# Down projection by Strassen's seven products, and matmuls issued as 64-column halves, in a long-convolution and gated-MLP kernel

## The chip, the cores and the metric

The kernel runs on one core of one Trainium2 chip. The metric is device time in microseconds (us) of one execution; lower is better. A core has a matrix engine (PE, with its weight loads shown as PEld), VectorE (DVE), ScalarE (ACT), GpSimd (POOL) and SyncE (SP), which here only starts DMA transfers. The engines run their own instruction queues in order and meet through semaphores. PE reads from SBUF and writes to PSUM, which has eight banks of 512 float32 columns on 128 partitions; POOL does not touch PSUM in this kernel.

## What is computed

```python
batch, seq, d_model, filter_order = 4, 12480, 128, 64
...
h_filt = (np.maximum(pos_emb @ w1, 0.0) @ w2) * np.exp(-0.01 * pos)[:, None]
u = x * v
y = irfft(rfft(u, n=2*S) * rfft(h_filt, n=2*S))[:, :S, :]
z = (x * y).reshape(B * S, D)            # 49920 tokens of 128 channels
h = z @ w_in                             # w_in: 128 x 2048
return (h * np.cos(h)) @ w_out           # w_out: 2048 x 128
```

Everything is float32 (the two large weights arrive as float64 and are converted on the chip). The first half is a causal convolution of each channel with a long filter; the second is an MLP with the activation h·cos(h).

## The kernel before

The convolution is made of small Fourier matrices, in five kinds of work per batch element: the product u = x·v and its even and odd sums (`u_multiply`, `u_sums`, on POOL in the middle of the kernel), a forward stage (`f1_mm`, line 410), a second stage with the product by the filter's transform (`f2_mm`, line 451, and `f2_product`, lines 474 to 477), an inverse stage (`i1_mm`, line 482) and a last one (`i2_mm`, line 507), whose result `i2_out` multiplies by x and stores to a scratch array `zd` in DRAM. The filter's own transform and batch element 0 as far as `i1` are done first, alone.

From then on the MLP and the convolution are interleaved by hand (`manual_schedule`: each queue has the order in which the code issues). The tokens are cut into 98 row groups (`NALL`), 512 tokens each but for the first and the last, and the 2048 hidden channels into 16 chunks of 128 (`NFC`). One step of the main loop is one chunk of one row group: 1568 steps. Step i issues, in this order:

- `moe_up`: one matmul of 128 weight columns by 512 tokens into a PSUM tile `ph` (line 746), then on ACT the rounding to whole turns, `k` (line 749), and on DVE the remainder `f` (line 751);
- `moe_down` for step i − LAG: one matmul of 512 tokens that adds to the accumulator `acc` (line 768, also shown as `cv` when the accumulator lies in a bank of the convolution);
- `moe_act` for step i − 1: the sine on ACT (`cs`, line 757) and the product with `ph` on DVE (`gt`, line 759). This is the last reader of that step's `ph`;
- at some steps: `moe_turn` (four transposes of the next row group's tokens, line 129, through a `ph` tile and an ACT copy, line 740), `moe_back` (four transposes of the result, line 129, through a `ph` tile and the ACT copy `ob`, line 783), loads and stores;
- then as much work of the convolution as the accounting in `owed` asks for: every step adds 1, every yield of the convolution costs its own number of steps.

Each float32 matmul is recorded as two matmul records and two weight loads; a transpose as one of each. In the main loop PSUM holds four `ph` tiles (`ps_h`), one accumulator and three banks of the convolution (`ps_c`). The steps after the convolution's end are called the tail here.

Where the last stage of one batch element runs (`inverse_units`), the products u of the next one are made beside it. `u_units` has a pool of `bufs` buffers for x and `bufs − 1` for v (`xt`, `vt`); the load of a tile waits until POOL has multiplied the tile that held its buffer. SP's one queue issues these loads, the loads of `tm` and `xs` for the last stage, the stores to `zd`, the loads `zb` of the MLP and the stores of the result, all in program order.

Of the kernel before, what the change touches and what calls it, by code (L numbers as in the profile page):

```python
# [33 lines left out]
def kernel(  # L34
# [74 lines left out]
    LAG = 4  # L109
# [15 lines left out]
    tw_w = const.tile([KE, 2, N1], F32, name="tw_w")  # L125

# [26 lines left out]
    def float32_join(dst, raw, power, high):  # L153
# [6 lines left out]
        if dst.space == DRAM:  # L160
# [5 lines left out]
                 for c in range(0, DFF, WCOL)]  # L166
    out_pieces = [(slice(c, c + WCOL // D), out_words[:, c:c + WCOL // D, :, :])
                  for c in range(0, NFC, WCOL // D)]
# [239 lines left out]
    def f1_mm(ps, u, b, i):  # L408

        nc.tensor.matmul(ps[0:KE, i * 2 * N1:(i + 1) * 2 * N1], u[:, b, 0:KE, i],  # L410
                         c1[0:u.shape[0], :, :].rearrange("p r k -> p (r k)"),
                         start=True, stop=True)
# [32 lines left out]
    def f2_mm(ps, w, k1, i, filt=False):  # L445
# [4 lines left out]
        if not filt:  # L450
            nc.tensor.matmul(pi, w[:, i, :], parts[0:KE, :, k], start=True, stop=True)  # L451
        elif k < KF:
            both = ftile[0:KE, :, k:k + N1 + 1:N1, :].rearrange("p b r i -> p r b i")
            nc.tensor.matmul(pi, w[:, i, :], both, start=True, stop=True)
        else:
            for r, src in enumerate((ftile[0:KE, :, k, :], above[0:KE, :, k - KF, :])):
                nc.tensor.matmul(pi[:, r], w[:, i, :], src, start=True, stop=True)  # L457
# [22 lines left out]
    def i1_mm(ps, b, i):  # L480
        for r in range(2):
            nc.tensor.matmul(  # L482
                ps[0:N1, (i * 2 + r) * N2:(i * 2 + r + 1) * N2],
                parts[0:N2, r, :, b, i],
                cs[:, r, :], start=True, stop=True)
# [10 lines left out]
    def i2_mm(ps, t, g, part):  # L496
        for i in range(part * G // 2, (part + 1) * G // 2):
# [8 lines left out]
            for r, place in enumerate(places):  # L506
                nc.tensor.matmul(ps[0:R, i * D:(i + 1) * D], t[:, i, r, :],  # L507
                                 slots[0:N1, :, place, :], start=(r == 0), stop=(r == 1))

    def i2_out(pool, ps, xs, b, g):  # L510
        if b == 0:
            yield
        zs = pool.tile([R, 2, UA, D], F32, name="zs")
        nc.vector.tensor_tensor(
            zs[:, :, :, :].rearrange("p h n d -> p (h n d)"), ps[0:R, :],
            xs[:, :, :].rearrange("p h n -> p (h n)"), op=ALU.mult)
        z = zs[:, :, :, :].rearrange("p h n d -> p (h n) d")
# [150 lines left out]
    def i2_units(bank, b, bufs):  # L668

        with tc.tile_pool(name="back", bufs=2, side="left" if b else "right") as pool:  # L670
            ts, xss = {}, {}

            def before(j):
                ts[j] = pool.tile([N1, G, 2, R], F32, name="tm", bufs=bufs)
                xss[j] = pool.tile([R, 2, UA * D], F32, name="xs", bufs=bufs)
# [15 lines left out]
    def inverse_units(bank, b):  # L691
# [6 lines left out]
        new = u_units(b + 1, 3, slots[0:R, :, :, :],  # L698
# [20 lines left out]
    ats, accs = {}, {}  # L719
# [7 lines left out]
    def moe_load(pool, n):  # L727
        m, row = rows_of(n), first_row(n)
        zb = pool.tile([P, G, D], F32, name="zb", bufs=2)
# [13 lines left out]
    def moe_up(pool, n, c):  # L743
        m = G * rows_of(n)
        ph = ps_h.tile([P, BANK], F32, name="ph")
        nc.tensor.matmul(ph[:, 0:m], w_in_sb[:, c * P:(c + 1) * P], ats[n][:, 0:m],  # L746
                         start=True, stop=True)
        k = pool.tile([P, BANK], I32, name="k")
        nc.scalar.activation(k[:, 0:m], ph[:, 0:m], AF.Identity, bias=TURNS[c % 4][0])  # L749
        f = pool.tile([P, BANK], F32, name="f", bufs=3)  # L750
        nc.vector.scalar_tensor_tensor(out=f[:, 0:m], in0=ph[:, 0:m],  # L751
                                       scalar=TURNS[c % 4][0], in1=k[:, 0:m], op0=ALU.add, op1=ALU.subtract)
        return ph, f, m, TURNS[c % 4][1] * TWO_PI

    def moe_act(pool, ph, f, m, scale):
        cs = pool.tile([P, BANK], F32, name="cs")
        nc.scalar.activation(cs[:, 0:m], f[:, 0:m], AF.Sin, scale=scale)  # L757
        gt = pool.tile([P, BANK], F32, name="gt", bufs=4)
        nc.vector.tensor_tensor(gt[:, 0:m], ph[:, 0:m], cs[:, 0:m], op=ALU.mult)  # L759
        return gt  # L760

    def moe_down(n, c, gt):
        if c == 0:

            accs[n] = bank() if made[0] == B * NG and n % 2 else \
                ps_acc.tile([P, BANK], F32, name="acc")
        m = G * rows_of(n)
        nc.tensor.matmul(accs[n][:, 0:m], w_out_sb[:, c, :], gt[:, 0:m],  # L768
                         start=(c == 0), stop=(c == NFC - 1))

    def moe_evict(pool, n):
        m = G * rows_of(n)
        ot = pool.tile([D, BANK], F32, name="ot", bufs=1)
        nc.scalar.copy(out=ot[:, 0:m], in_=accs.pop(n)[:, 0:m])
        return ot

    def moe_back(pool, n, ot):
        m = rows_of(n)
        pt = ps_h.tile([P, BANK], F32, name="ph")
        for i in range(G):  # L780
            transpose(pt[0:m, i * D:(i + 1) * D], ot[:, i * m:(i + 1) * m], ident)
# [18 lines left out]
    with tc.manual_schedule():  # L800
        with tc.tile_pool(name="psum", bufs=8, space=PSUM) as psum, \
# [96 lines left out]
            for kept, here in ((rowsd, rows), (twd, tw_t)):  # L898
# [4 lines left out]
            w_out_sb = wpool.tile([P, NFC, D], F32, name="w_out_sb")  # L903
            nc.sync.dma_start(w_in_sb[:, :], wind[:, :])
            beside(i1_units(bank), [(w_out_sb[:, c, :], w) for c, w in out_pieces], 2.0 * math.pi,
                   some_groups)

        ps_acc = ctx.enter_context(tc.tile_pool(name="ps_acc", bufs=1, space=PSUM))
        ps_h = ctx.enter_context(tc.tile_pool(name="ps_h", bufs=4, space=PSUM))
# [24 lines left out]

        conv = convolutions()
# [11 lines left out]
        hidden, gates, ots, obs = {}, {}, {}, {}  # L947
        for i in range(len(steps) + LAG):
            if i < len(steps):
# [5 lines left out]
                hidden[i] = moe_up(mpool, n, c)  # L955
            if i >= LAG:
                pn, pc = steps[i - LAG]
                moe_down(pn, pc, gates.pop(i - LAG))
                if pc == NFC - 1:
                    ots[pn] = moe_evict(mpool, pn)  # L960
            if 0 <= i - 1 < len(steps):
                gates[i - 1] = moe_act(mpool, *hidden.pop(i - 1))
# [41 lines left out]
```

## Time and profile before

| what | us |
|---|---|
| median of 3 runs | 3737.86 (3736.82 to 3740.14) |
| the profiled execution's own time | 3736.99 |
| its span, first to last instruction | 3734.9 |

Busy time by stretch of the span, in us; the granted TensorE clock is 1.00 in all of them and 0.995 over the span:

| stretch | what runs beside the MLP | PE | DVE | POOL |
|---|---|---|---|---|
| 340 to 600 | last stage of element 0, u of element 1 | 259.36 | 192.04 | 97.43 |
| 600 to 740 | forward stage | 140.00 | 106.41 | 1.47 |
| 740 to 1040 | second stage and product | 300.00 | 251.32 | 69.58 |
| 1040 to 1180 | inverse stage | 140.00 | 102.10 | 0.00 |
| 1180 to 1400 | last stage of element 1, u of element 2 | 219.81 | 140.96 | 86.54 |
| 1990 to 2210 | last stage of element 2, u of element 3 | 220.00 | 141.15 | 86.61 |
| 2660 to 2940 | inverse and last stage of element 3 | 280.00 | 185.19 | 0.00 |
| 2940 to 3730 | nothing: the tail | 789.74 | 577.54 | 0.00 |

Busy time of matmuls counts from the start of a record to its modelled end, so overlapping records are merged; how densely PE works is read from the distance between the starts of two records.

### The profile page before, as it was taken

Reading aid. Unit: us, or ns where it says so; the run is one execution under the profiler, and the core shown is the slowest. Engines: PE = TensorE matmul, PEld = TensorE weight load, DVE = VectorE, ACT = ScalarE, POOL = GpSimd, SP = SyncE. Lnnn points to the kernel's source line nnn. Section 1 sums busy time; section 2 is a strip of 40 time slices with the busy share of each in tenths; the row PEclk is TensorE's granted clock in tenths of the full one; section 3 lists DMA queues with packets and bytes.
Section 4 is the critical chain, followed back from the end, with each engine's and each line's share of the span. In section 5 each row is a group of like instructions: output and inputs, shape, how many; then the busy total and the mean of one; then the engine's idle time right before and its main releaser. Section 6 shows DMA issues by size and latency. Waiting matters only on the chain.

```text
span 3734.9 us, 46660 instructions
## 1 busy us (share of the span) xinstructions
PE 3681.9 (99%) x13546; PEld 2109.8 (56%) x13546; DVE 2805.7 (75%) x5330; ACT 2294.6 (61%) x4660; POOL 714.6 (19%) x1005
## 2 busy tenths in 40 slices
PE   8898999999999999999999999999999999999999
PEld 6777555555566556555565556555666544444444
DVE  8887777788876667788876667888775677777776
ACT  5757666655555557655555567655554566666666
POOL 6666340022201430122102420122000000000000
PEclk9999999999999999999999999999999999999999
DMA  5263551022203650122104630122106200000000
GB/s 168 65 184 114 159 163 38 25 76 76 67 17 95 177 149 12 47 74 79 49 18 136 182 102 16 56 80 76 40 15 182 68 23 17 17 23 18 18 21 15
DMA packets 209494, 276.10 MB, mean 74 GB/s; under 512 B 17111, under 2 KB 146535, under 8 KB 209111
## 3 DMA queue, kind: packets, MB, share of 16 engines
q1 hardware_dynamic: 209239, 273.12, 25.0%
q8 instruction: 109, 1.79, 0.2%
q14 instruction: 146, 1.20, 0.1%
HBM read 193.64 MB, written 79.42 MB: 73 GB/s over the span
## 4 chain that ended last, share of the span: by engine, by line
PE 95%; DVE 1%; DMA 1%; ACT 1%; POOL 1%; issue 1%; SPq 0%; DVEq 0%; ACTq 0%; POOLq 0%
PE ph L746 36%; PE acc L768 31%; PE cv L507 6%; PE cv L768 5%; PE cv L482 4%; PE cv L451 3%; PE cv L410 3%; PE ph L129 2%; PE ps L410 2%; PE ps L451 1%; PE ps L482 1%; DMA wd<-w 1%; DVE slots L492 0%; PE ps L457 0%; DVE ftile L367 0%
## 5 line engine op out<-in xcount | busy, mean ns | idle before, releaser
L749 ACT ACTIVATE k<-ph 128x512 int32<-128x512 f32 (+1 forms) x1568 | 932.8, 595 | 1237.0 <-PE ph L746 1236.5
L751 DVE SCALAR_TENSOR_TENSOR f<-ph,k 128x512 f32<-128x512 f32 (+1 forms) x1568 | 1080.1, 689 | 792.8 <-ACT k L749 779.5
L746 PE MATMUL ph<-at,w_in_sb 128*128 128x512 f32 (+1 forms) x3136 | 1596.2, 590 | 0.6 <-ACT at L740 0.6
L768 PE MATMUL acc<-gt,w_out_sb 128*128 128x512 f32 (+1 forms) x2688 | 1369.4, 591 | 0.0
L759 DVE TENSOR_TENSOR gt<-ph,cs 128x512 f32<-128x512 f32 (+1 forms) x1568 | 1064.1, 679 | 60.5 <-ACT cs L757 60.4
L757 ACT ACTIVATE cs<-f 128x512 f32<-128x512 f32 (+1 forms) x1568 | 973.2, 621 | 0.6 <-DVE f L751 0.6
L768 PEld LDWEIGHTS acc<-gt,w_out_sb 128*128 128x128 f32 x2688 | 508.0, 189 | 642.4 <-issue 630.0
L746 PEld LDWEIGHTS ph<-at,w_in_sb 128*128 128x128 f32 x3136 | 553.6, 190 | 330.7 <-issue 239.8
L477 POOL TENSOR_TENSOR slots<-slots,t 120x256 f32<-120x256 f32 x384 | 281.1, 738 | 1149.2 <-DVE t L476 623.1
L507 PEld LDWEIGHTS cv<-slots,tm 96*104 96x104 f32 x1920 | 239.2, 169 | 100.2 <-issue 86.2
L398 POOL TENSOR_TENSOR xt<-xt,vt 104x256 f32<-104x256 f32 x228 | 165.8, 747 | 514.5 <-DMA vt<-in_v_dram 513.3
L507 PE MATMUL cv<-slots,tm 96*104 96x128 f32 x1920 | 251.5, 273 | 5.2 <-POOL tm L300 5.0
L768 PE MATMUL cv<-gt,w_out_sb 128*128 128x512 f32 (+1 forms) x448 | 224.0, 583 | 0.0
L482 PEld LDWEIGHTS cv<-cs,slots 120*96 120x96 f32 x1536 | 176.6, 167 | 67.1 <-issue 65.2
L482 PE MATMUL cv<-cs,slots 120*96 120x120 f32 x1536 | 183.1, 266 | 0.0
L404 POOL TENSOR_TENSOR slots<-xt 104x256 f32<-104x256 f32 x210 | 157.2, 756 | 94.1 <-PE cv L507 78.2
L451 PEld LDWEIGHTS cv<-slots,w 124*120 124x120 f32 x576 | 103.6, 184 | 124.3 <-issue 110.2
L451 PE MATMUL cv<-slots,w 124*120 124x256 f32 x576 | 173.0, 380 | 0.0
L410 PEld LDWEIGHTS cv<-c,slots 104*124 104x124 f32 x768 | 132.7, 192 | 64.8 <-issue 61.0
L410 PE MATMUL cv<-c,slots 104*124 104x192 f32 x768 | 150.8, 326 | 0.0
L768 PEld LDWEIGHTS cv<-gt,w_out_sb 128*128 128x128 f32 x448 | 85.0, 190 | 103.2 <-issue 99.5
L492 DVE TENSOR_TENSOR slots<-cv,other 96x240 f32<-96x240 f32 x384 | 132.9, 393 | 1.4 <-ACT other L490 1.1
(129 smaller groups left out, 2307.4 us busy)
## 6 DMA issues: line engine op xcount, KB each, us to landing
h<-hd SPq DMA_DIRECT2D x144, 240.0 KB
tm<-td SPq DMA_DIRECT2D x96, 312.0 KB
xt<-in_x_dram SPq DMA_DIRECT2D x120, 208.0 KB
vt<-in_v_dram SPq DMA_DIRECT2D x120, 208.0 KB
xs<-in_x_dram SPq DMA_DIRECT2D x120, 208.0 KB
zd<-zs SPq DMA_DIRECT2D x119, 208.0 KB
zb<-zd SPq DMA_DIRECT2D x96, 256.0 KB
w<-wd SPq DMA_DIRECT2D x144, 116.2 KB
```

The source lines that it names most:

```text
L398: engine.tensor_tensor(xt[:, half, :], xt[:, half, :], vt[:, half, :], op=ALU.mult)
L410: nc.tensor.matmul(ps[0:KE, i * 2 * N1:(i + 1) * 2 * N1], u[:, b, 0:KE, i], c1[0:u.shape[0], :, :].rearrange("p r k -> p (r k)"), start=Tr ...
L451: nc.tensor.matmul(pi, w[:, i, :], parts[0:KE, :, k], start=True, stop=True)
L477: nc.gpsimd.tensor_tensor(y[:, r], y[:, r], t[:, r], op=op)
L482: nc.tensor.matmul(ps[0:N1, (i * 2 + r) * N2:(i * 2 + r + 1) * N2], parts[0:N2, r, :, b, i], cs[:, r, :], start=True, stop=True)
L507: nc.tensor.matmul(ps[0:R, i * D:(i + 1) * D], t[:, i, r, :], slots[0:N1, :, place, :], start=(r == 0), stop=(r == 1))
L746: nc.tensor.matmul(ph[:, 0:m], w_in_sb[:, c * P:(c + 1) * P], ats[n][:, 0:m], start=True, stop=True)
L749: nc.scalar.activation(k[:, 0:m], ph[:, 0:m], AF.Identity, bias=TURNS[c % 4][0])
L751: nc.vector.scalar_tensor_tensor(out=f[:, 0:m], in0=ph[:, 0:m], scalar=TURNS[c % 4][0], in1=k[:, 0:m], op0=ALU.add, op1=ALU.subtract)
L757: nc.scalar.activation(cs[:, 0:m], f[:, 0:m], AF.Sin, scale=scale)
L759: nc.vector.tensor_tensor(gt[:, 0:m], ph[:, 0:m], cs[:, 0:m], op=ALU.mult)
L768: nc.tensor.matmul(accs[n][:, 0:m], w_out_sb[:, c, :], gt[:, 0:m], start=(c == 0), stop=(c == NFC - 1))
```

## The change

The down projection no longer multiplies each chunk by all 128 output channels and 512 tokens. Two chunks are taken together, and the 2 × 2 blocks (two chunks by two halves of the channels, two chunks by two halves of the tokens) are multiplied by Strassen's seven products instead of eight. The sums of weights are made once, on POOL; the sums of the gated tokens (`moe_sums`) on POOL for each pair of chunks; the sums of the results when the accumulators are emptied (`moe_evict`, now in two halves). Each product has 64 weight columns and 256 tokens and is issued as two matmuls of 128 tokens that write partitions 0 to 63 and 64 to 127. In the main loop every other matmul, those of the convolution and the up projection, is also issued as two matmuls of at most 64 columns; the inverse stage's 96 rows become 97, so that its second half has 33. The transposes stay whole. The accumulators take two banks, so `ps_h` has three; after the convolution's end every other `ph` tile lies in one of its banks. The lag from up to down grows from 4 to 6 steps, the loads of u have one buffer less, and some tiles are worked on in place.

```diff
-    LAG = 4
+    LAG = 6
...
+    def mm(dst, left, right, start=True, stop=True):
+        n = dst.shape[0]
+        for lo, hi in ((0, CB), (CB, n)) if tiled[0] else ((0, n),):
+            nc.tensor.matmul(dst[lo:hi], left[:, lo:hi], right, start=start, stop=stop)
...
-            nc.tensor.matmul(
-                ps[0:N1, (i * 2 + r) * N2:(i * 2 + r + 1) * N2],
-                parts[0:N2, r, :, b, i],
-                cs[:, r, :], start=True, stop=True)
+            n = max(N1, CB + CB // 2 + 1) if tiled[0] else N1
+            mm(ps[0:n, (i * 2 + r) * N2:(i * 2 + r + 1) * N2],
+               slots[0:N2, b, r * N1:r * N1 + n, i], cs[:, r, :])
...
-                xss[j] = pool.tile([R, 2, UA * D], F32, name="xs", bufs=bufs)
+                xss[j] = pool.tile([R, 2, UA * D], F32, name="xs", bufs=bufs + 1)
...
-        new = u_units(b + 1, 3, slots[0:R, :, :, :],
+        new = u_units(b + 1, 2, slots[0:R, :, :, :],
...
-        zb = pool.tile([P, G, D], F32, name="zb", bufs=2)
+        zb = pool.tile([P, G, D], F32, name="zb", bufs=1)
...
-        ph = ps_h.tile([P, BANK], F32, name="ph")
-        nc.tensor.matmul(ph[:, 0:m], w_in_sb[:, c * P:(c + 1) * P], ats[n][:, 0:m],
-                         start=True, stop=True)
+        late = made[0] == B * NG and c % 2
+        ph = bank() if late else ps_h.tile([P, BANK], F32, name="ph")
+        mm(ph[:, 0:m], w_in_sb[:, c * P:(c + 1) * P], ats[n][:, 0:m])
...
+    def moe_sums(pool, n, gt):
+
+        half = G // 2 * rows_of(n)
+        ts = pool.tile([P, 4, BANK // 2], F32, name="ts")
+        t = [ts[:, i, 0:half] for i in range(4)]
+        b11, b21 = gt[:, 0, 0:half], gt[:, 1, 0:half]
+        nc.gpsimd.tensor_tensor(
+            ts[:, 0:2, 0:half], gt[:, :, half:2 * half],
+            gt[:, 0, 0:2 * half].rearrange("p (h n) -> p h n", h=2), op=ALU.subtract)
+        nc.gpsimd.tensor_tensor(t[2], t[1], b11, op=ALU.add)
+        nc.gpsimd.tensor_tensor(t[3], b21, t[2], op=ALU.subtract)
+        return b11, b21, gt[:, 1, half:2 * half], t
+
+    def moe_down(n, pair, second, b11, b21, b22, t):
+
+        r = rows_of(n)
+        if pair == 0:
+            sums[n, second] = ps_acc.tile([P, 4, P], F32, name="acc" + "ab"[second])
+        acc = sums[n, second]
+        todo = ((3, 6, b22), (0, 1, t[1]), (1, 4, t[0]), (2, 3, t[3])) if second else \
+            ((0, 0, b11), (2, 2, b21), (1, 5, t[2]))
+        for i, (place, weight, right) in enumerate(todo):
+            for h in range(2):
+                nc.tensor.matmul(acc[h * CB:(h + 1) * CB, place, 0:r],
+                                 w_out_sb[:, pair, weight, :], right[:, h * r:(h + 1) * r],
+                                 start=(pair == 0 and i == 0), stop=(pair == NFC // 2 - 1),
+                                 skip_group_check=True)
...
+        if not second:
+            ot = pool.tile([P, 6, P], F32, name="ot", bufs=1)
+            nc.scalar.copy(out=ot[:, 2, 0:r], in_=acc[:, 0, 0:r])
+            nc.vector.tensor_tensor(ot[:, 0:2, 0:r], acc[:, 1:3, 0:r], twice(ot[:, 2, 0:r]),
+                                    op=ALU.add)
+            return ot
+        nc.vector.tensor_tensor(ot[:, 2:4, 0:r], acc[:, 0:2, 0:r], twice(ot[:, 0, 0:r]),
+                                op=ALU.add)
+        nc.vector.tensor_tensor(ot[:, 4:6, 0:r], acc[:, 2:4, 0:r], ot[:, 2:4, 0:r], op=ALU.add)
+        nc.vector.tensor_tensor(ot[:, 0, 0:r], acc[:, 1, 0:r], ot[:, 2, 0:r], op=ALU.add)
         return ot
...
+            for dst, first_, second_, op in ((4, 1, 3, ALU.add), (5, 4, 0, ALU.subtract),
+                                             (1, 0, 1, ALU.subtract), (6, 2, 5, ALU.subtract)):
+                nc.gpsimd.tensor_tensor(w_out_sb[:, :, dst, :], w_out_sb[:, :, first_, :],
+                                        w_out_sb[:, :, second_, :], op=op)
...
-        ps_h = ctx.enter_context(tc.tile_pool(name="ps_h", bufs=4, space=PSUM))
+        ps_h = ctx.enter_context(tc.tile_pool(name="ps_h", bufs=3, space=PSUM))
...
+        tiled[0] = True
...
-                moe_down(pn, pc, gates.pop(i - LAG))
-                if pc == NFC - 1:
-                    ots[pn] = moe_evict(mpool, pn)
+                moe_down(pn, pc // 2, pc % 2, *gates[i - LAG - pc % 2])
+                if pc >= NFC - 2:
+                    ots[pn] = moe_evict(mpool, pn, pc % 2, ots.get(pn))
             if 0 <= i - 1 < len(steps):
-                gates[i - 1] = moe_act(mpool, *hidden.pop(i - 1))
+                moe_act(*hidden.pop(i - 1))
+                pn, pc = steps[i - 1]
+                if pc % 2:
+                    gates[i - 2] = moe_sums(mpool, pn, pairs.pop(i - 2))
```

`f1_mm`, `f2_mm` and `i2_mm` call `mm` in place of `nc.tensor.matmul` and are otherwise as before. `moe_back` transposes four blocks of `ot` into places that put the channel halves together again.

## The prediction

> **What bounds the kernel now.** I read the share of each engine first, then the chain that ended last, then the order of events in the tail, then the stretches.
>
> ```profile
> PE 3681.9 (99%) x13546; PEld 2109.8 (56%) x13546; DVE 2805.7 (75%) x5330; ACT 2294.6 (61%) x4660; POOL 714.6 (19%) x1005
> ...
> PE 95%; DVE 1%; DMA 1%; ACT 1%; POOL 1%; issue 1%; SPq 0%; DVEq 0%; ACTq 0%; POOLq 0%
> PE ph L746 36%; PE acc L768 31%; PE cv L507 6%; PE cv L768 5%; PE cv L482 4%; PE cv L451 3%; PE cv L410 3%; PE ph L129 2%; PE ps L410 2%; PE ps L451 1%; PE ps L482 1%; DMA wd<-w 1%; DVE slots L492 0%; PE ps L457 0%; DVE ftile L367 0%
> ```
>
> PE is the bound: it never waits in the main loop, and the down projection (L768, as acc and cv) is 36% of the chain, as much as the up projection. The timeline of PE in the tail shows how densely it works:
>
> ```profile
> 3003.23 1.02 PE L746 MATMUL ph<-at,w_in_sb 128*128 128x512 f32 x2
> 3004.09 1.02 PE L768 MATMUL cv<-gt,w_out_sb 128*128 128x512 f32 x2
> 3004.95 0.60 PE L129 MATMUL ph<-ident,zb 128*128 128x128 f32 x4
> 3005.39 1.02 PE L746 MATMUL ph<-at,w_in_sb 128*128 128x512 f32 x2
> ```
>
> The first column is the start. A float32 matmul of 512 columns takes 0.86 us from its start to the next one's, 0.429 per record; a transpose of 128 columns 0.44/4 = 0.110. A record's modelled duration is 0.592 (mean of L746), so 0.16 us of each lies under its successor. A step of up and down is 2 x 0.858 = 1.717 us.
>
> The stretches, in columns PE, PEld, DVE, ACT, POOL, show where another engine is near. They are: u made beside the last stage; the forward stage; the second stage; the tail.
>
> ```profile
> 1180.00:1400.00 220.00, 219.81 (x875) 125.90 (x874) 140.96 (x222) 116.81 (x211) 86.54 (x121) 1.00 0.57 167
> 1400.00:1550.00 150.00, 150.00 (x533) 91.23 (x532) 114.60 (x223) 103.95 (x228) 2.22 (x3) 1.00 0.06 18
> 1550.00:1840.00 290.00, 290.00 (x852) 149.31 (x851) 243.47 (x473) 170.23 (x309) 68.77 (x93) 1.00 0.25 73
> 2940.00:3730.00 790.00, 789.74 (x2024) 363.47 (x2022) 577.54 (x901) 540.36 (x984) 0.00 (x0) 1.00 0.07 18
> ```
>
> **The change, part by part.** *Seven products.* For a pair of chunks PE had two down matmuls, 4 x 0.429 = 1.716 us. It now has 7 x 2 = 14 matmuls of 64 columns by 128 tokens, 28 records of 0.109 (the transposes, and 0.111 for the 128-token records of L507 below): 3.05 us one after the other, 1.526 if the two halves stream side by side. No row of before has two matmuls at once, so the trace bounds this from both sides: −0.19 us a pair, x 784 pairs = −149 us, or +1.34 x 784 = +1050. The same question hangs on the up projection (0 or +0.858 x 1568 = +1345) and the convolution's halves (0 or at most +758, the summed busy time of L507, L482, L410 and L451 of cv). I take side by side, −149: two halves use separate columns and partitions, and the weight loads, which are already hidden under 0.102 us records at 96 columns, become shorter. No row shows which side is nearer; this is a judgement.
>
> *Transposes stay whole.* Four times per row group, 392 times, PE changes between 64-column halves and the whole array. Bounds: nothing, or the 0.16 us tail plus a weight load of 0.19 (L746's PEld) bare each time, 0.35. I take 0.25, 98 us, of which some 40% falls into the waits below: +60 (0 to 137).
>
> The page "TensorEngine Tiling (Array Packing)" of the Trainium skill, section Key Properties, says that changing the tiling mode drains TensorE; no row of before shows such a change, and by that rule alone the zero end would fall away.
>
> *Three ph tiles instead of four.* With an up at 2999.80, its gt ends at 3004.56 (3003.88 + 0.68): the tile is held for 4.76 us, 2.8 steps, because gt stands on DVE behind the next step's f. Three tiles cover three steps (5.15), but twice per row group four transposes take one of them. In the order up A, transposes, up B, up C, C needs A's tile and is due 2 x 1.717 + 0.44 = 3.87 us after A: it waits 0.9. In the changed program's order the up behind the result's transposes even waits, in 68 of 98 row groups, for the copy of those same transposes (0.16 of tail and 0.58, L783), which comes to about as much. The wait holds all of PE, including the convolution queued behind. Before the tail there are 1118 steps, 70 row groups, 140 such places: 126 us bare. Work of the convolution issued in between (on average 0.5 us a step: 2585 us from the first up at 355 to 2940, by 1118 steps, less 1.77 with transposes) covers part, and some places lie in stretches that POOL sets. I take +80 (0 to 140). The tail has six tiles and pays nothing.
>
> *Sums on POOL.* A 128x256 POOL operation is 0.728 (L150) to 0.738 (L477); 512 columns are not shown, between one and two of these; by the slope from 0.623 to 0.640 at 208 columns (L300) about 1.28. A pair costs 1.28 + 2 x 0.74 = 2.76 us (2.2 to 2.95), 1.38 a step. In the tail that is 2.76 of 3.4 us: hidden. In the second stage POOL has 69 + 139 x 1.38 = 261 of 290: just hidden. Where u is made, POOL has 87 + 96 x 1.38 = 219 of 220, and 97 + 119 x 1.38 = 262 of 260: full at the old pace. The 311 steps of these three stretches gain nothing: 311 x 0.095 = +30. And what waits there waits in POOL's queue ahead of the sums:
>
> ```profile
> 1254.43 1.42 POOL L398 TENSOR_TENSOR xt<-xt,vt 104x256 f32<-104x256 f32 x2 [2.87 <-DMA vt<-in_v_dram]
> ...
> 1256.17 0.46 SPq L379 DMA_DIRECT2D vt<-in_v_dram  x1
> 1256.85 1.05 PE L507 MATMUL cv<-slots,tm 96*104 96x128 f32 x8
> ...
> 1261.10 1.41 POOL L398 TENSOR_TENSOR xt<-xt,vt 104x256 f32<-104x256 f32 x2 [2.60 <-DMA vt<-in_v_dram]
> ```
>
> Already now v's load is issued when the last product is done (1256.17) and the next product starts 4.93 us later, on its landing, every 6.7 us. With one buffer less, and 4.1 us of sums per such round queued on POOL around those products, the round becomes 4.9 + 0.4 of issue + 1.4 of products + part of the sums, 7 to 8 us. Behind the waiting product stand the sums, for which PE's down waits; behind the waiting load on SP stand xs, tm (for which L507 waits), zd and zb. 90 rounds x 0 to 1.1 us: +50 (0 to 100).
>
> *Emptying the accumulators.* Per row group ACT's copy of 512 (0.585, L774) becomes one of 128, and DVE gets three operations of 256 columns (0.415, L476) and one of 128 (about 0.28 by the same slope): 1.5 us, 0.10 a step. In the tail DVE has 0.68 + 0.69 + 0.10 = 1.47 of a step of 1.7; it hides under PE and would cost its 150 us only if DVE became the bound. The four weight sums come once, before the first down needs them, and lag 6 delays only the end, by POOL's chain and the longer emptying: +5.
>
> **Sum:** 3734.9 − 149 + 30 + 60 + 80 + 50 + 5 = 3811; with the 2.1 us outside the span (3736.99) and 0.9 to the median, **3814 us**, slower by 2%. Its own range is 3745 to 3900.
>
> **The rivals.** *Faster, 3670.* One mechanism: PE keeps the saving because its waits are covered. It needs the ph waits and width changes nearly free: the convolution's work between ups already fills 0.5 of the 0.9 us, and a width change at 0.1 us costs 39. 3738 − 149 + 30 + 39 + 10 = 3668. It decides once ph waits, width changes and POOL together cost less than about 140. For it: everything else is off the chain. Against it: nothing in the two timelines stands between a transpose and the next up where no convolution is due.
>
> *Halves start in order, 4200.* In before every record starts after the one ahead of it in the program. A matmul is two records, so the second half of an up (429 ns records) runs on while the first half's column group has finished; if a record may not start before the one ahead, a following product half of 0.109 waits 0.429 − 0.109 = 0.32 us, each step: 1568 x 0.32 = 502. PE would be slower, so POOL and ph waits shrink to some 80 with the width changes: 3738 − 149 + 502 + 80 = 4171, and up to 4250.
>
> The page "TensorE: Matmul & The Clock Gate" of the Trainium skill, Part 3, section "What overlaps and what doesn't", speaks for this: matmuls start and end in program order and only weight loads are pulled ahead; the same section reports tiles running concurrently. By its order rule the sum is the 4171 just given, by free column groups 3814. No run here shows either.
>
> *The array does not share.* If small matmuls need the 0.102 us that the tightest load-and-matmul pair shows (L482), each half by itself: 28 x 0.102 = 2.86 for 1.716, +896, and L507 and L482 doubled, 1920 x 0.111 + 1536 x 0.102 = +370: 5000. If nothing streams side by side: 3738 + 1050 + 1345 + 758 = about 6900.
>
> **Numbers.** Slower as summed 0.38; faster 0.29; in between, no measurable change, 0.05; in order 0.17; not shared 0.11. So faster 0.29, same 0.05, slower 0.66, where 0.2% is about what a measurement of this kernel can tell. The time is the likeliest case's. The range leaves out what is under 3655 and over 4200.
>
> **What would show it.** In the tail: starts of two ups 3.2 to 3.4 us apart per pair would confirm sharing, 3.9 the order, over 5 neither. Around L129's records: an idle of PE before and after. At PE's waits: ups waiting for DVE's gt, before the tail only. In 1180 to 1400: POOL above 95% and PE idle, waiting for ts. I am wrong in kind if PE's pair takes longer than 3.43 in the tail, and wrong in size if waits for ph are absent.

## The result and the profile after

| | us | against before |
|---|---|---|
| before, median of 4 runs | 3738.61 (3736.82 to 3740.14) | |
| after, median of 4 runs | 3947.86 (3946.23 to 3959.36) | 1.0566, 95% interval 1.0545 to 1.0587 |
| after, span of the profiled execution | 3947.6 | |

The change costs 209 us. The page of the changed kernel, engine shares and the chain by engine:

```profile
PE 3703.9 (94%) x40298; PEld 2595.6 (66%) x40298; DVE 2903.3 (74%) x5722; ACT 2281.0 (58%) x4660; POOL 2838.1 (72%) x3361
...
PE 67%; POOL 11%; DMA 5%; DVE 5%; issue 2%; ACT 1%; SPq 1%; POOLq 0%; ACTq 0%; DVEq 0%
```

In after, line 132 is the helper `mm` and 785 the seven products; 768, 771 and 772 are the sums on POOL; 754 makes `f`, 760 is the product `gt`; 404 multiplies x by v, 410 makes the sums of u, 481 and 482 are the second stage's product with the filter.

PE had 99% of the span and 95% of the chain. It now has 94% and 67%, so it waits; POOL has gone from 19% of the span to 72%, and with DMA it takes 16% of the chain.

Where the time went is read by stage. A stage begins with the first matmul of its kind in the trace; the numbers are the distances to the next stage's first matmul, in us, and "last" runs from element 3's last stage to the last up, so it holds the tail. The later rows are the experiments below.

| kernel | u made beside the last stage, three times | second stage, three times | forward and inverse stages, all six | last | median |
|---|---|---|---|---|---|
| before | 250 / 229 / 236 | 296 / 293 / 294 | 858 | 933 | 3739 |
| after | 271 / 288 / 299 | 324 / 319 / 322 | 856 | 919 | 3948 |
| e1, before in halves | 259 / 238 / 244 | 306 / 303 / 303 | 870 | 957 | 3829 |
| e3, before with three ph | 262 / 237 / 244 | 314 / 310 / 309 | 877 | 1004 | 3905 |
| e2, after without the sums | 260 / 233 / 240 | 305 / 301 / 301 | 847 | 918 | 3754 |
| e4, after, three sets of u | 272 / 286 / 297 | 324 / 319 / 321 | 856 | 917 | 3947 |
| e6, after, two buffers of t | 271 / 294 / 296 | 306 / 302 / 302 | 856 | 918 | 3897 |
| e7, after, u's products on DVE | 284 / 266 / 266 | 324 / 321 / 321 | 849 | 914 | 3903 |
| e10, after, tm from ACT's queue | 271 / 264 / 268 | 324 / 320 / 322 | 855 | 911 | 3881 |
| e11, t and tm | 271 / 260 / 270 | 306 / 302 / 301 | 856 | 911 | 3829 |
| e12, t, tm, products on DVE | 271 / 280 / 274 | 305 / 302 / 302 | 851 | 911 | 3848 |
| e13, the same and a fourth ph | 270 / 253 / 261 | 338 / 332 / 325 | 1173 | 911 | 4213 |
| e15, t, tm, three sets of u | 270 / 238 / 246 | 305 / 302 / 301 | 856 | 911 | 3781 |
| e16, the same, products on DVE | 270 / 236 / 243 | 305 / 302 / 301 | 853 | 911 | 3772 |
| e9, seven products in the tail only | 255 / 229 / 236 | 297 / 293 / 294 | 859 | 917 | 3730 |
| e14, e9 with lag and buffers as before | 255 / 229 / 236 | 296 / 293 / 294 | 859 | 917 | 3730 |

After loses 143 us in the stages where u is made (858 − 715) and 82 in the second stages (965 − 883); the forward and inverse stages together and the last part are faster.

The tail shows the products themselves. The timeline of PE there, ups and downs:

```profile
3502.30 1.03 PE L132 MATMUL ph<-at,w_in_sb 128*64 128x512 f32 x4
3503.16 0.61 PE L785 MATMUL acca<-gt,w_out_sb 128*64 128x128 f32 x8
3503.59 0.39 PE L785 MATMUL acca<-ts,w_out_sb 128*64 128x128 f32 x4
3503.81 1.03 PE L132 MATMUL cv<-at,w_in_sb 128*64 128x512 f32 x4
3504.67 0.39 PE L785 MATMUL accb<-gt,w_out_sb 128*64 128x128 f32 x4
3504.89 0.82 PE L785 MATMUL accb<-ts,w_out_sb 128*64 128x128 f32 x12
3505.54 1.03 PE L132 MATMUL ph<-at,w_in_sb 128*64 128x512 f32 x4
```

The first column is the start. An up of two halves takes 0.86 us, as one whole matmul did, and the 28 product records 0.65 + 0.87 = 1.52 us: two halves do stream side by side. A pair of chunks takes 3505.54 − 3502.30 = 3.24 us instead of 3.43. The saving is real, and it is the stages with the convolution that give it back.

The waits there, first in the stage where element 2's u is made (1216 to 1504), with total us, times and the longest:

```profile
PEld cv L132 <- DMA tm<-td: 39.9, 18, 4.9
POOL ts L768 <- PE accb L785: 37.7, 21, 4.8
PE cv L132 <- DMA tm<-td: 35.6, 18, 4.6
...
POOL xt L404 <- DMA vt<-in_v_dram: 23.2, 13, 2.6
```

and in a second stage (748 to 1072):

```profile
DVE t L481 <- POOL slots L482: 36.7, 33, 2.6
POOL ts L768 <- PE accb L785: 35.5, 34, 2.4
...
PE ph L132 <- DVE gt L760: 16.5, 22, 1.6
```

The same two kinds of stage in before, 1180 to 1400 and 740 to 1040, have no wait for `tm` and none of DVE for POOL among their longest. The longest of each:

```profile
POOL xt L398 <- DMA vt<-in_v_dram: 234.2, 29, 164.4
```

```profile
POOL slots L477 <- DVE t L476: 203.7, 91, 3.8
```

In the first stage of after, PE stands for a load of the last stage's matrices, which SP issues in order behind the loads of x and v; in the second, DVE stands for POOL in the product with the filter, where POOL had waited for DVE before, and PE stands for DVE's last read of a `ph` tile. POOL itself is not full: the stretches, with the columns PE, PEld, DVE, ACT, POOL, then the granted clock:

```profile
1240.00:1500.00 260.00, 219.32 (x2480) 156.91 (x2476) 139.23 (x232) 108.92 (x198) 198.23 (x246) 0.95 0.47 132
1640.00:1940.00 300.00, 280.74 (x2844) 176.15 (x2840) 237.26 (x481) 162.79 (x294) 243.84 (x289) 1.00 0.24 68
```

POOL has 198 of 260 and 244 of 300 us, while PE stands idle for 41 and 19. So the question for the experiments was whether POOL's work is too much or only stands in the wrong order.

### The profile page after: what moved, and what is told of

Same layout as the page of the kernel before. It is cut to its first block, busy times and chain, and to the rows that moved or that the text cites. A ratio compares the mean times of both kernels' runs of the same rounds, so it can differ in the third digit from the quotient of the medians.

```text
span 3947.6 us, 101170 instructions
## 1 busy us (share of the span) xinstructions
PE 3703.9 (94%) x40298; PEld 2595.6 (66%) x40298; DVE 2903.3 (74%) x5722; ACT 2281.0 (58%) x4660; POOL 2838.1 (72%) x3361
## 4 chain that ended last, share of the span: by engine, by line
PE 67%; POOL 11%; DMA 5%; DVE 5%; issue 2%; ACT 1%; SPq 1%; POOLq 0%; ACTq 0%; DVEq 0%
PE ph L132 23%; PE cv L132 18%; PE accb L785 14%; PE acca L785 10%; DMA tm<-td 4%; POOL ts L768 4%; PE ph L136 2%; POOL ts L771 2%; POOL ts L772 2%; DVE gt L760 2%; DVE gt L754 1%; POOL xt L404 1%; POOL slots L482 1%; POOL slots L410 1%; ACT gt L753 1%
## 5 line engine op out<-in xcount | busy, mean ns | idle before, releaser
L753 ACT ACTIVATE gt<-ph 128x512 int32<-128x512 f32 (+1 forms) x1339 | 797.7, 596 | 1347.3 <-PE ph L132 1231.3
L768 POOL TENSOR_TENSOR ts<-gt 128x512 f32<-128x512 f32 (+2 forms) x784 | 998.4, 1273 | 791.4 <-PE accb L785 737.1
L754 DVE SCALAR_TENSOR_TENSOR gt<-ph,gt 128x512 f32<-128x512 f32 (+1 forms) x1339 | 918.9, 686 | 791.1 <-ACT gt L753 779.3
L132 PE MATMUL ph<-at,w_in_sb 128*64 128x512 f32 (+1 forms) x5356 | 1414.0, 601 | 78.6 <-DVE gt L760 56.8
L759 ACT ACTIVATE gt<-gt 128x512 f32<-128x512 f32 (+1 forms) x1568 | 973.8, 621 | 32.1 <-DVE gt L754 32.1
L760 DVE TENSOR_TENSOR gt<-ph,gt 128x512 f32<-128x512 f32 (+1 forms) x1339 | 907.4, 678 | 0.3
L785 PE MATMUL accb<-ts,w_out_sb 128*64 128x128 f32 (+2 forms) x9408 | 655.1, 273 | 0.0
L772 POOL TENSOR_TENSOR ts<-gt,ts 128x256 f32<-128x256 f32 (+2 forms) x784 | 571.1, 728 | 61.5
L771 POOL TENSOR_TENSOR ts<-ts,gt 128x256 f32<-128x256 f32 (+2 forms) x784 | 570.6, 728 | 61.5
L785 PEld LDWEIGHTS accb<-ts,w_out_sb 128*64 128x64 f32 x9408 | 549.3, 138 | 0.0
```

Of the source, the lines that this page charges most:

```text
L132: nc.tensor.matmul(dst[lo:hi], left[:, lo:hi], right, start=start, stop=stop)
L753: nc.scalar.activation(turns, ph[:, 0:m], AF.Identity, bias=phase)
L754: nc.vector.scalar_tensor_tensor(out=part, in0=ph[:, 0:m], scalar=phase, in1=turns, op0=ALU.add, op1=ALU.subtract)
L759: nc.scalar.activation(part, part, AF.Sin, scale=scale)
L760: nc.vector.tensor_tensor(part, ph, part, op=ALU.mult)
L768: nc.gpsimd.tensor_tensor(ts[:, 0:2, 0:half], gt[:, :, half:2 * half], gt[:, 0, 0:2 * half].rearrange("p (h n) -> p h n", h=2), op=ALU.sub ...
```

## The experiments

### What each part costs by itself

**e1: halves alone.** Before, with every matmul of the main loop cut in two, eight products and four `ph` tiles as they were.

```diff
...
-        nc.tensor.matmul(ph[:, 0:m], w_in_sb[:, c * P:(c + 1) * P], ats[n][:, 0:m],
-                         start=True, stop=True)
+        mm(ph[:, 0:m], w_in_sb[:, c * P:(c + 1) * P], ats[n][:, 0:m])
...
-        nc.tensor.matmul(accs[n][:, 0:m], w_out_sb[:, c, :], gt[:, 0:m],
-                         start=(c == 0), stop=(c == NFC - 1))
+        mm(accs[n][:, 0:m], w_out_sb[:, c, :], gt[:, 0:m],
+           start=(c == 0), stop=(c == NFC - 1))
```

> The kernel before, with every matmul of the main loop (down too) issued as two halves of at most 64 columns and nothing else changed: eight products, lag 4, four ph tiles, no sums. It prices the halves and the changes of width around the transposes. Width theory, from the changed kernel's tail (0.245 us more around each of 196 groups of transposes than their 0.109 pitch): 3738 + 48 = 3786, and a tail step of 1.78 against 1.751 before. If the halves themselves cost anything on PE, above 3800; if the width changes explain the result, about 3940.

Measured: 3828.82 us (3826.0 to 3829.8), ratio 1.0237 (1.0222 to 1.0253), +89 us. In its tail a step takes 1.7880 us against 1.7515, which is 0.58 us for each row group of 16 steps with its two groups of transposes; over all 1568 steps that makes 57 us. The other 32 us lie in the stages with the convolution, whose matmuls are halves too. What makes those dearer was not tried.

**e3: three ph tiles alone.** Before, with `bufs=3` for `ps_h`.

```diff
-        ps_h = ctx.enter_context(tc.tile_pool(name="ps_h", bufs=4, space=PSUM))
+        ps_h = ctx.enter_context(tc.tile_pool(name="ps_h", bufs=3, space=PSUM))
```

> The kernel before with three ph tiles instead of four. My forecast's term: up to 0.9 us at 140 places before the tail, and in the tail, which has no other tiles here, at another 56: 3738 + 80 to 180 = 3820 to 3920. If the convolution's work covers the waits, 3738 to 3780, the tail alone.

Measured: 3904.5 us (3903.5 to 3905.55), ratio 1.0441 (1.0425 to 1.0457), +164 us. A tail step takes 1.9019 us; 458 x 0.1504 = 69 us of the loss is in the tail, which the changed kernel doesn't pay, since its ups use the convolution's banks there. Ahead of it 95 us are lost. The group of the ups' weight loads, with busy time, mean ns, and then the idle time before it, first in before, then here:

```profile
L746 PEld LDWEIGHTS ph<-at,w_in_sb 128*128 128x128 f32 x3136 | 553.6, 190 | 330.7 <-issue 239.8 <-DVE gt L759 15.9 <-DVE t L476 13.9
L746 PEld LDWEIGHTS ph<-at,w_in_sb 128*128 128x128 f32 x3136 | 548.5, 189 | 496.7 <-issue 155.7 <-DVE gt L759 124.1 <-ACT at L740 107.4
```

The tile comes free by DVE's `gt`, or is one that transposes hold until ACT's copy `at`: the two waits that were expected.

**e2: no sums.** After, where the products read parts of `gt` and the three POOL operations of `moe_sums` are gone.

```diff
-        nc.gpsimd.tensor_tensor(
-            ts[:, 0:2, 0:half], gt[:, :, half:2 * half],
...
-        nc.gpsimd.tensor_tensor(t[2], t[1], b11, op=ALU.add)
-        nc.gpsimd.tensor_tensor(t[3], b21, t[2], op=ALU.subtract)
-        return b11, b21, gt[:, 1, half:2 * half], t
+        return b11, b21, gt[:, 1, half:2 * half], [b11, gt[:, 0, half:2 * half], b21, b11]
```

> The changed kernel without the sums of gated tokens: the products read slices of gt in their place, so POOL has none of its 2140 us of new work; all 14 matmuls of a pair, the three ph tiles and the single u buffer stay. POOL theory: the stretches where u is made and the second stages lose their 59 and 27 us each, so 3948 - 225 = 3723 or, with the saving of 0.095 a step that comes back there, down to 3660 to 3690. Ph theory (three tiles hold PE): it stays above 3850.

Measured: 3753.92 us (3747.77 to 3758.8), ratio 1.0041 (1.0028 to 1.0053). The sums cost 3948 − 3754 = 194 us, of which 125 in the stages where u is made and 58 in the second stages. All the rest of the change together is +15 us. Nine tenths of the loss is therefore due to the sums. They do not make DVE's own work longer: `gt` (line 760) takes 678 ns in after as without the sums, and 679 in before.

### Why the sums cost that much

**e4: the third set of u buffers back.**

```diff
-        new = u_units(b + 1, 2, slots[0:R, :, :, :],
+        new = u_units(b + 1, 3, slots[0:R, :, :, :],
```

> The changed kernel with the loads of u on three buffers of x and two of v, as before. If the single v buffer makes SP's queue wait and tm late (PE waited 36 to 38 us for tm in each of two such stretches), those stretches give back most of their 59 us: 3948 - 100 = about 3850. If POOL's work alone fills them (1.38 us a step of sums beside 88 us), they stay near 280 us: 3930 to 3950.

Measured: 3947.42 us (3942.96 to 3952.84), ratio 1.0556 (1.0541 to 1.0572): nothing. Taken alone, the buffer that the change removed is not the cause. This did not yet show that it is harmless; e15 shows that it is not.

**e6: two buffers for t.** In the second stage's product POOL adds `t` to `slots` (line 482) and frees it; DVE can't write the next `t` before. POOL's addition now stands behind 2.7 us of sums.

```diff
-        t = pool.tile([N2, 2, CB, 4], F32, name="t", bufs=1 + whole)
+        t = pool.tile([N2, 2, CB, 4], F32, name="t", bufs=2)
```

> The changed kernel with two buffers for the tile t of the second stage's products instead of one, so that VectorE no longer waits there for GpSimd (108.2 us of waits in the profile of the changed kernel). If that wait is what makes the second stages 26 to 28 us longer than before, they fall by some 15 us each and the kernel to about 3900 us. If GpSimd's own work, queued in order, is the limit, VectorE's wait goes and PE's waits stay: 3940 to 3950 us, and second stages of 319 to 324 us as now.

Measured: 3896.98 us (3892.07 to 3899.2), ratio 1.0424 (1.0409 to 1.044), 51 us less. The second stages come back to 306, 302 and 302, about what they take with no sums at all (305, 301, 301). The waits in one of them (749 to 1055):

```profile
PEld ph L132 <- DVE gt L760: 6.5, 9, 0.9
```

DVE's wait for POOL is gone from the list, and the ups' wait for `gt` is small. POOL does the same work there in less time, 262 of 306 us: it was never the limit, only a queue in which a small operation stood behind large ones.

**e7: u's products on DVE.**

```diff
         new = u_units(b + 1, 2, slots[0:R, :, :, :],
-                      lambda j, half: nc.gpsimd,
+                      lambda j, half: nc.vector,
```

> The changed kernel with u's products x*v (two a round, 0.73 us each on GpSimd) on VectorE in the two stages where u is made beside the tokens' work, and in the rest as it is. GpSimd is relieved of 60 rounds x 1.46 = 88 us in these stages (VectorE was busy for 139 of 260 us there). If GpSimd's load is what makes these stages 59 to 63 us longer than before, they come back to 235 to 250 us each and the kernel to about 3850 us. If the loads' order in SyncE's queue is the cause, the wait for tm stays at some 30 us a stage: 3920 to 3950 us.

Measured: 3903.25 us (3897.0 to 3906.41), ratio 1.0441 (1.0425 to 1.0456). The edit moves the products in all three stages. It gives half of what the theory of a full POOL asked for: the two later stages fall to 266, not to 235 to 250, and the first rises from 271 to 284. In the second of the three DVE now waits 34.7 us for v. Neither theory is met.

**e10: tm's loads from ACT's queue.**

```diff
-                nc.sync.dma_start(ts[j][:, :, :, :], td[j, :, :, :, :])
+                nc.scalar.dma_start(ts[j][:, :, :, :], td[j, :, :, :, :])
```

> The changed kernel with the loads of tm issued from ScalarE's queue instead of SyncE's, where they stand behind loads of x and v whose buffers GpSimd holds. If SyncE's order is what keeps PE waiting (36 to 41 us in each of the two later stages where u is made), these waits go and the kernel falls to 3860 to 3880 us. If GpSimd's work is the limit, the wait only changes its name (PE waits for the sums or for u instead) and the time stays at 3930 to 3950 us.

Measured: 3881.18 us (3880.1 to 3885.89), ratio 1.0386 (1.0371 to 1.0402), 67 us less, nearly all that SP's order was expected to give. The waits in the same stage as above, now 1215 to 1479:

```profile
PEld acca L785 <- POOL ts L771: 20.1, 11, 3.4
PE acca L785 <- POOL ts L771: 17.3, 9, 3.2
POOL xt L404 <- DMA vt<-in_v_dram: 16.0, 9, 2.8
POOL ts L768 <- PE accb L785: 11.1, 6, 4.8
```

PE no longer waits for `tm`. What it waits for now is the sums, half as long, and POOL still stands for v.

**e11: both repairs,** the diffs of e6 and e10 together.

> The changed kernel with both repairs that helped in the stages: two buffers for t, and tm's loads from ScalarE's queue. Alone they gave 51 and 67 us. If they mend different places (second stages; stages where u is made), they add up: 3825 to 3835 us. If both only shift the same lack of GpSimd time, the sum is well under 118 us: 3850 us or more.

Measured: 3829.09 us (3828.37 to 3834.39), ratio 1.0247 (1.0233 to 1.0261). 51 and 67 add up, 3948 − 118 = 3830, to within the spread of the runs. They mend two places that don't touch: the table has e6's second stages and, nearly, e10's stages where u is made.

**e12: both, and u's products on DVE in the later two stages.**

```diff
-                      lambda j, half: nc.gpsimd,
+                      lambda j, half: nc.vector if b else nc.gpsimd,
```

> As the run with both repairs, and u's products on VectorE in the later two of the three stages where u is made. If what is left there (264 and 268 us, against 233 and 240 with no sums) is GpSimd being late with the sums, these two fall to 240 to 250 us and the kernel to 3785 to 3805 us, some 40 us above the run without sums (3754). If it is VectorE's or the loads' turn to be late, nothing is gained: 3825 us or more.

Measured: 3848.11 us (3843.52 to 3850.65), ratio 1.0293 (1.0279 to 1.0307): 19 us lost where some 35 were to be won. The waits in the stage from 1200 to 1480:

```profile
DVE xt L404 <- DMA vt<-in_v_dram: 57.0, 23, 3.9
...
POOL ts L768 <- DVE gt L760: 28.1, 12, 3.2
PE ph L132 <- DVE gt L760: 25.9, 20, 3.8
```

The wait for v went with the product to DVE, an engine on which every step depends: `gt` stands behind it, then the ups and the sums. POOL has 180 us of work in 280, so time on POOL was not what was short.

**e15: both repairs and three sets of u,** the diffs of e4, e6 and e10. What differs from e11 is that v is loaded a round ahead, and POOL's work is the same.

> As the run with both repairs (3829 us), and three sets of u tiles instead of two, which loads v a round earlier. In the changed kernel alone the third set gave nothing; there PE stood behind tm's loads. If GpSimd's waits for v (22 us in a stage where u is made) are what is left of the loss there, these stages fall from 260 and 270 to 240 to 250 us and the kernel to 3785 to 3805 us. If GpSimd's own time is the limit (225 us of work in 260), its idle time only moves: 3815 to 3830 us.

Measured: 3780.88 us (3780.19 to 3782.33), ratio 1.0115 (1.01 to 1.013), 48 us under e11. The edit that gave nothing in e4 gives 48 us after the other two. That it is `tm` that had hidden its worth is argued: in e4 PE still waits 36 us for `tm` in the second of the three stages, and `t` is used in other stages. The two later stages take 238 and 246 us, 6 and 7 more than with no sums, with POOL busy for 216 of 238. The waits in the first of them (1200 to 1440), and after it the page's chain:

```profile
POOL ts L768 <- PE accb L785: 13.0, 10, 4.8
...
PEld cv L132 <- POOL slots L410: 5.0, 2, 4.6
```

```profile
PE 82%; DVE 4%; ACT 2%; POOL 2%; issue 1%; DMA 1%; ACTq 0%; SPq 0%; POOLq 0%; DVEq 0%
```

No wait for v or `tm` is on this list any more, and POOL has fallen from 11% of the chain to 2%. The 4.6 us are one wait at the stage's end, where the forward stage needs POOL's last sum of u; it makes up most of what is left there. The first of the three stages is not mended by anything tried here: 270 to 272 us with the loads moved or not, 284 in e7, 260 without the sums. In e15 it ends in such a wait of 7.1 us, with POOL busy for 248 of 271.

**e16: the same, and u's products on DVE in the later two stages,** the diffs of e15 and e12.

> As the run with three changes, u's products on VectorE (3848 us), and three sets of u tiles. VectorE waited 57 us for v in a stage there, and ups and sums behind it. If that wait was why moving the products lost 19 us, it goes and GpSimd has 185 us of work in a stage: 235 to 250 us for each of the two stages and 3775 to 3805 us in all. If VectorE is late with something else, 3830 us or more.

Measured: 3772.3 us (3770.62 to 3773.12), ratio 1.0091 (1.0074 to 1.0108). With v there in time, the edit that lost 19 us gains 9, and DVE's 57 us of waits for v are not among the longest waits of the same stage any more. The wait for v was why e12 lost.

### Can it be made to win?

**e13: a fourth ph tile from the convolution's third bank,** on top of e12; every fourth up takes it.

```diff
...
-                        tc.tile_pool(name="ps_c", bufs=3, space=PSUM))
+                        tc.tile_pool(name="ps_c", bufs=2, space=PSUM))
+                    fourth.append(stack.enter_context(
+                        tc.tile_pool(name="ps_4", bufs=1, space=PSUM)))
```

> As the run with three changes, and from the second convolution on the third bank of the convolution's results goes to a fourth tile for every fourth up. The kernel before lost 164 us when its fourth tile was taken away, some 90 of them ahead of the tail. If the missing tile costs the changed kernel as much, it gets some 40 to 60 us back here (only the later two of three rounds of stages have it): 3730 to 3760 us, about the kernel before. If with lag 6 and three tiles the ups lose little, or the convolution needs its third bank as much, 3790 to 3810 us.

Measured: 4213.36 us (4205.46 to 4215.1), ratio 1.1267 (1.1252 to 1.1283), far outside both. The later two stages where u is made gain 27 and 13 us over e12 by the tile, but each forward and inverse stage loses 50 to 60 us and each second stage 20 to 30. The waits of the first forward stage (607 to 798):

```profile
PEld cv L132 <- ACT slots L423: 24.8, 21, 1.6
PE cv L132 <- DVE slots L425: 22.7, 15, 2.3
```

The bank is gone in all three rounds of forward, second and inverse stages, which the expectation had not counted, and with two banks PE waits for their emptying by ACT and DVE. Neither the `ph` tiles (e3, in the kernel before) nor the convolution's banks had one to spare, so the second accumulator had to be paid for somewhere. What the missing `ph` tile costs in the changed kernel itself can't be read from this run.

**e9: seven products in the tail alone.** Eight products, whole matmuls, one accumulator and four `ph` tiles until the convolution ends; then its banks become the second accumulator and two more `ph` tiles.

```diff
...
+                if c == 0 and made[0] == B * NG and not seven(n):
+                    for _ in conv:
+                        pass
+                    stack.close()
+                    more[:] = [stack.enter_context(tc.tile_pool(name=a, bufs=k, space=PSUM))
+                               for a, k in (("ps_m", 2), ("ps_b", 1))]
+                    first_seven[0] = n
+                    tiled[0] = True
...
```

> Eight products and whole matmuls, as before, as long as the convolution runs; from the first row group that begins after it, seven products and halves as in the changed kernel, with six tiles for ph, and lag and in-place tiles of the changed kernel throughout. If the loss lies all in the stages where convolution and tokens share GpSimd and the banks, the stages are as before and the last 450 steps take 1.70 us instead of 1.75: 3710 to 3718 us, under the kernel before. If lag or the in-place tiles cost time in the stages, it is above 3740 us.

Measured: 3729.87 us (3727.79 to 3731.7, 10 runs), ratio 0.998 (0.997 to 0.9989), 8 us under the kernel before, where 20 to 28 were expected: neither of the two outcomes that were named. Its tail takes 780 us instead of 802, as expected, but begins 13 us later: 5 of these are lost in the first stage where u is made, 6 in element 3's last stage.

**e14: e9 with the lag of 4, three sets of u and two `zb`, as before, until the tail.**

```diff
...
-            if i >= LAG:
-                pn, pc = steps[i - LAG]
+            while down[0] <= i - (LAG if i >= len(steps) or seven(steps[i][0]) else 4):
+                d = down[0]
+                down[0] += 1
+                pn, pc = steps[d]
...
```

> The version with seven products in the tail alone (3730 us), with the lag of 4 steps, three sets of u tiles and two of zb of the kernel before as long as the convolution runs. Its stages ended some 6 us later than before; if lag and buffers made that, 3722 to 3726 us; if it is the tiles in place, 3730 us again.

Measured: 3730.36 us (3726.86 to 3733.09, 11 runs), ratio 0.9978 (0.9969 to 0.9987): e9 again. Lag and buffers are not those 13 us. The tiles worked on in place are left as a suspect, not tried by themselves.

## Why the prediction was right or wrong

The direction was right, but the loss was 209 us and not 76. The time lies inside the wide range from 3655 to 4200, and outside the 3745 to 3900 that the sum gave itself. Of the 133 us by which the sum fell short, 114 belong to the sums on POOL: 194 by e2, 80 in the sum. Term by term:

**Seven products, −149: right.** 3.43 − 3.24 = 0.19 us a pair, x 784. The two rivals on the array, halves in order and an array that isn't shared, are out: a pair would take 3.9 us or over 5. The section of the Trainium skill that spoke for the first ("TensorE: Matmul & The Clock Gate", Part 3, "What overlaps and what doesn't") is not contradicted. It has matmuls start in program order, and here they do: the records of one up start at 3502.298, 3502.305, 3502.727 and 3502.734. A record does not say which half it belongs to; I read them as the first records of both halves, then the second ones. The mistake was mine, to read the rule as if one half's two records had to start before the other half's first; interleaved like this, order costs nothing.

**Width changes, +60: the size was about right, partly by luck, and not complete.** The timeline of PE in the tail around a group of transposes:

```profile
3511.38 0.82 PE L785 MATMUL accb<-ts,w_out_sb 128*64 128x128 f32 x12
3512.13 0.66 PE L136 MATMUL ph<-ident,zb 128*128 128x128 f32 x4
3512.72 1.08 PE L132 MATMUL ph<-at,w_in_sb 128*64 128x512 f32 x4
```

From the first transpose to the next up it is 0.59 us, where four took 0.44 before; with the wait ahead of the first one a group costs some 0.25 us more, 48 us over 196 groups, and e1's tail gives 57. A group has two changes, so one costs 0.12 to 0.15 us and not 0.25, and in the tail nothing of it falls into other waits, where the prediction had hidden 40%: two errors that cancel. That it costs something agrees with the drain at a change of tiling that the prediction cited. What the sum left out is the other 32 us that e1 loses where the convolution runs in halves.

**Three ph tiles, +80: near, as far as was measured,** 95 us ahead of the tail by e3, in the kernel before, within its bounds of 0 to 140. In the changed kernel it was not measured by itself; e2 leaves 75 us for it and the emptying together (3754 = 3739 − 149 + 89 + 75). "The tail pays nothing" held, with a tail step of 1.70 us after.

**Sums on POOL, +30 and +50: this is the step that failed.** The sums took the 1.28 us (1.273 measured) and 0.73 us that were worked out, and "in the second stage POOL has 261 of 290: just hidden" is right as a count of work (260 to 263 measured). But hidden was read from the total. POOL's queue is in order, and the first operation to be late is not a sum but the 0.74 us addition that frees DVE's single `t`. DVE waits for it, `gt` stands behind `t`, the `ph` tile stays taken, PE waits: 58 us by e2, 51 of them given back by one more buffer. The term for the second stages was zero.

In the stages where u is made the chain was named correctly (the product waits for v, the sums stand behind it on POOL, `tm` stands behind v's load on SP), but at 0 to 1.1 us a round it was priced too low: the sums cost 125 us there (e2) against the 80 of both terms. The 30 us rested on a POOL that is full. With `t`, `tm` and the u buffers mended, e15 has POOL 91% busy in the second of these stages and loses only 6 and 7 us to the sums in the later two, so their steps need not lose by POOL's work; the first, with 11 us left, was not cleared up. By difference of runs, `tm`'s place in SP's queue is 67 us and the loads one round ahead 48, the latter only after the other repairs.

**Nothing in the sum for the clock.** 17 stretches at half clock, 81.9 us in all, lie between 345 and 3720 in the trace of after, none in that of before and none in e2's. The prediction counted waits at their length; see the last section.

**The measured terms together:** 3739 − 149 + 89 + 95 + 194 = 3968, 20 above the 3948 measured. The overlap of `ph` waits with stages that POOL sets, which the prediction allowed for, is of that order, but this is argued and not measured.

**The rival that ended faster (3670)** needed `ph` waits, width changes and POOL under 140 together; they are 378 by the single runs. Its other half, that the stages could cover the waits, no run shows: e16, the best with seven products throughout, is still 34 us above the kernel before.

## What to carry to other kernels

That an engine has time for added work says nothing about what stands behind that work: list the small operations already in its in-order queue, and for each how many buffers its consumer has; here one more buffer, one load moved to another queue and one load issued earlier gave back 167 of 194 us without taking away any work. A repair that gives nothing alone (e4) can be worth 48 us after another one, and moving a waiting operation to a freer engine moves the wait too (e12). When a change needs a resource that one phase is short of, try it in the phase that has the resource to spare: here the seven products pay when they are used in the tail alone, though only by 0.2%.

## What the hardware showed that was not expected

After idle time of PE its matmuls can run at half speed for a while. The stage from 2111 to 2410 in after and part of the tail, by stretches as above:

```profile
2111.00:2410.00 299.00, 250.50 (x2863) 180.66 (x2859) 158.03 (x261) 123.65 (x225) 222.72 (x275) 0.94 0.46 130
3160.00:3900.00 740.00, 740.00 (x7991) 475.45 (x7989) 581.84 (x968) 520.23 (x945) 589.45 (x645) 1.00 0.08 21
```

After the five pairs of busy time and count stands the granted clock, 0.94 and 1.00. In the first there are seven stretches of 3.41 or 6.83 us at a clock of 0.5; 15 of after's 17 lie in the stages where u is made. One of them runs from 1363.0 to 1369.8, behind a wait of 2.79 us:

```profile
1363.66 1.97 PE L132 MATMUL cv<-slots,tm 96*64 96x128 f32 x16 [2.79 <-DMA tm<-td]
1365.39 1.94 PE L132 MATMUL ph<-at,w_in_sb 128*64 128x512 f32 x4
1367.09 1.09 PE L785 MATMUL acca<-gt,w_out_sb 128*64 128x128 f32 x8
```

The up takes 1.70 us to the next start instead of 0.86. An estimate from this: 81.9 us at half clock cost at most 41 us, less where PE was idle in them. No run separates this from the waits themselves; e15 has three such stretches with 23.9 us, and only three idle times of PE over 2 us after the first up, of 4.4 to 7.1 us, one ahead of each.

The Trainium skill's "TensorE: Matmul & The Clock Gate", Part 1, "What's actually happening", has the clock at half after an idle window of about 3.4 us, until a busy one has passed. The lengths agree, multiples of 3.41 us. But the window need not be wholly idle here: with after's trace from 400 to 3900 us cut into the windows of 3.41 us at whose borders the stretches begin, every window in which PE was idle for 2.1 us or more was followed by one at half clock. Between 1.7 and 2.1 us some were, and below that none, except behind a window that was at half clock already.

The other was how well column halves share the array: two halves of an up start 7 ns apart, and the up takes the 0.86 us of the whole matmul.
